# W and R loaded with two tokens of one batch per partition, and the order of the work written anew

## The chip, the cores and the metric

The kernel runs on one core of one Trainium2 chip. A core has five engines that each work through their own list of instructions: TensorE (PE; its weight loads are shown as PEld), VectorE (DVE), ScalarE (ACT), GpSimd (POOL) and SyncE (SP), which here only starts transfers. The metric is the device time of one execution in microseconds (us).

## The reference

The reference is a linear-attention recurrence with a decaying state, followed by a two-layer network with a squared ReLU. For each of 4 batches and 8 heads, with 768 tokens of 40 channels:

```python
for t in range(S):
    y[:, :, t] = np.einsum('bhd,bhde->bhe', rt, state)
    Sa = np.einsum('bhde,bhe->bhd', state, at)
    state_decay = state * wt[:, :, None, :] - np.einsum('bhd,bhe->bhde', Sa, bt)
    state = state_decay + np.einsum('bhd,bhe->bhde', vt, kt)
# x: y with the 8 heads side by side, 3072 tokens x 320
h = x @ w_in                  # 320 x 2048
r = np.maximum(h, 0.0)
out = (r * r) @ w_out         # 2048 x 320
```

Inputs and output are float32.

## The kernel before

The 768 tokens are cut into 6 chunks of 128. A *batch* in the kernel's sense, `m` from 0 to 23, is one chunk of one of the four input batches, with all 8 heads; `m` and `m + 1` with `m` even make a *pair*. A *step* `st` from 0 to 47 is half a batch (4 heads). Inside a chunk the recurrence is solved with matrix products.

**Preparation of a batch** (`add_prep`, L315 to L526). Six loads (W, K, B, A, V, R), from batch 4 on one DMA for a pair (`two`, L296): token t lies on partition t, and each descriptor brings the 40 floats (160 bytes) of one token and head. For batches 0 to 3, R comes in another layout (`rows`, L301), so its transposed copy is read with strides when it is moved out of PSUM (`e_r`, L516). Then:

- `ln` (ACT, L321) takes the logarithm of W into a tile of its own, `hi` scales it by 512 into another, and `lo` takes the float32 minus its upper 16 bits. `cs` (PE, `sums` at L331) forms the sums of the logarithms over the tokens up to each token: two products with a 128 x 128 triangle, one with the upper halves and one with `lo`. `GI` and `GA` (ACT, L356) are the exponentials of minus and plus that sum.
- `E` is `GA` one token earlier. Up to batch 5 (`THREE = 6`) it comes from a second pair of products (`ce`) and an exponential; after that two DMAs shift `GA` by one partition.
- `GL` is the last row of `GA` turned into a column. Up to batch 5 (`GLD = 6`) four one-column products (`gl`, L374) put it into the bank of the sums, and DVE multiplies it out; after that a transposing DMA per pair does it (`gD`, L384), and POOL or DVE multiplies.
- `kb` and `aa` scale K, B and A; `cast` brings V and R to bfloat16; PE turns A, V and R (`tA`, `tV`, `tR`; from batch 8 on K and B are turned by DMA), and ACT or DVE moves each turned block out of PSUM (`AT`, `VT`, `RT`).

**A step** (`add_step`, L539): `ca` (64-row products, L563), masking by DVE (`CN`, L571, twice), `P`, `corr1`, `corr2` with small moves between them (`Mc`, `c1`, `Sn`), `tb`, `ex` (64-row products, L641), masking by DVE (`EVX`, L646, twice), `y` and `Xn`; `us` and `UZ` carry the state to the next chunk.

**The network** (`add_ff`, L800), per batch for the first four and per pair after that: `tx` turns the result, `hr` (64-row, L841) and `hp` (L854) multiply by `w_in`, `hs` applies the ReLU, `Gt` the square, `op` (L888) multiplies by `w_out`, `osb` moves the output, `st` stores it.

**The order.** Nothing is scheduled at run time. The kernel lists its operations, and four tables at the end fix the rest: `ORDER` (L960 on) is the order in which all operations are issued, and so each engine's list; `WAYS` says which of its possible engines an operation uses; `BANKS` gives the PSUM banks; `IDLE` (L1028) names operations of PE ahead of which products without use are put (L1060), in places where PE would otherwise stand idle. Each engine works strictly in order. Ahead of the listed work stand a few clearings of buffers on DVE and POOL (L160 to L209); the other clearings (`blank`, L182) are operations in the list.

## Time and profile before

| what | value |
|---|---|
| median of three runs | 258.16 us (256.76, 258.16, 258.46) |
| time of the profiled execution | 256.97 us |
| its span, first to last instruction | 255.4 us |
| busy PE / DVE / ACT / POOL | 242.0 / 230.4 / 215.6 / 172.0 us |
| granted TensorE clock | 1.000 |
| DMA packets; of these under 512 bytes | 172256; 165047 |

Busy times count an instruction from its start to its modelled end, so neighbours on a pipelined engine overlap: PE's 242.0 us are not 242.0 us of full use. A row of the timeline gives the start, the length from the first start to the last end, the engine and line, the tiles and the count; a row of the groups ends with the busy time, the mean length in nanoseconds and the idle time ahead of the group with what ended it. Starts can be compared directly, and the distance from one start to the next is what an instruction costs its engine when it is never kept waiting.

### The profile page before, as it was taken

How to read it: one execution, taken by the hardware profiler on the slowest of the kernel's cores; microseconds unless marked ns; L12 is line 12 of the kernel's file. 1: busy time of each engine (PE TensorE's matmuls, PEld its weight loads, DVE VectorE, ACT ScalarE, POOL GpSimd, SP SyncE). 2: the span in 40 equal slices, each digit the busy share in tenths (PEclk: the TensorE clock that was granted, in tenths of full speed). 3: DMA queues.
4: the chain of work that ended last, by engine and by line, in shares of the span. 5: the costliest groups of instructions: out<-in, count | busy, mean ns of one | idle time of the engine just before them, and what ended most of it. 6: DMA issues, size and time to landing. Idle time of an engine off the chain costs nothing.

```text
span 255.4 us, 9993 instructions
## 1 busy us (share of the span) xinstructions
PE 242.0 (95%) x3948; PEld 193.1 (76%) x3948; DVE 230.4 (90%) x556; ACT 215.6 (84%) x589; POOL 172.0 (67%) x259
## 2 busy tenths in 40 slices
PE   7978889999999999999999999999999999999993
PEld 7656667787787687887788777877788787878772
DVE  6799999998799999999999999999998898999482
ACT  3669978898698898899999999998999798877660
POOL 4366784886696969875568979995748694716340
PEclk9999999999999999999999999999999999999999
DMA  6999999999599979889988899988898989300111
GB/s 111 189 176 149 174 217 177 147 153 215 101 150 192 168 134 181 173 153 165 200 159 165 160 190 173 167 176 156 154 168 123 214 188 152 70 30 5 68 35 68
DMA packets 172256, 37.95 MB, mean 149 GB/s; under 512 B 165047, under 2 KB 170679, under 8 KB 172206
## 3 DMA queue, kind: packets, MB, share of 16 engines
q1 hardware_dynamic: 169646, 34.66, 76.5%
q0 software_dynamic: 2560, 2.62, 6.2%
q8 instruction: 31, 0.51, 0.9%
q14 instruction: 19, 0.16, 0.2%
HBM read 28.84 MB, written 3.93 MB: 128 GB/s over the span
## 4 chain that ended last, share of the span: by engine, by line
PE 51%; ACT 2%; DVE 2%; DMA 2%; issue 1%; POOL 0%; SPq 0%; POOLq 0%; DVEq 0%
PE bank L888 16%; PE bank L854 10%; PE bank L417 4%; PE bank L641 3%; PE bank L841 3%; PE bank L563 3%; PE bank L595 2%; PE bank L661 2%; DMA NA<-in_a_dram 2%; PE bank L333 1%; PE bank L669 1%; PE bank L623 1%; PE bank L816 1%; PE bank L586 1%; PE bank L628 1%
## 5 line engine op out<-in xcount | busy, mean ns | idle before, releaser
L646 DVE TENSOR_TENSOR EVX<-bank,MEX 128x512 bf16<-128x512 f32 x96 | 62.4, 683 | 1.6 <-PE bank L641 1.1
L571 DVE TENSOR_TENSOR CN<-bank,MCN 128x512 bf16<-128x512 f32 x96 | 61.3, 682 | 1.9 <-PE bank L563 1.0
L888 PE MATMUL bank<-WOUT,Gt 128*128 128x320 bf16 x384 | 59.4, 300 | 0.4 <-DMA WOUT<-in_moe_w_out_dram 0.4
L872 POOL TENSOR_TENSOR Gt<-hs 128x512 bf16<-128x512 bf16 x43 | 45.2, 1055 | 19.2 <-ACT hs L861 14.0
L854 PE MATMUL bank<-XT,WIN 128*128 128x256 bf16 (+1 forms) x448 | 54.5, 258 | 0.0
L861 ACT ACTIVATE hs<-bank 128x512 bf16<-128x512 f32 x77 | 45.5, 601 | 6.0 <-issue 2.5
L888 PEld LDWEIGHTS <-Gt 128*128 128x128 bf16 x384 | 35.4, 97 | 13.3 <-issue 0.8
L854 PEld LDWEIGHTS <-WIN 128*128 128x128 bf16 x448 | 34.8, 97 | 7.1 <-issue 3.6
L612 ACT ACTIVATE junk<-CN 128x512 bf16<-128x512 bf16 x48 | 30.6, 638 | 0.2
L341 POOL TENSOR_TENSOR lo<-hi 128x320 f16<-128x320 f32 x21 | 15.1, 720 | 15.0 <-ACT hi L237 8.5
L401 POOL TENSOR_TENSOR KB<-NB,GI 128x320 bf16<-128x320 f32 (+1 forms) x22 | 18.7, 854 | 8.3 <-ACT GI L357 6.8
L870 ACT ACTIVATE Gt<-hs 128x512 bf16<-128x512 bf16 x37 | 23.1, 636 | 1.4 <-DVE hs L863 1.4
L595 PEld LDWEIGHTS <-CN 128*128 128x128 bf16 x384 | 18.5, 96 | 5.3 <-issue 2.6
L401 POOL TENSOR_TENSOR KB<-NK,GI 128x320 bf16<-128x320 f32 x21 | 18.6, 888 | 5.5 <-ACT GI L357 5.5
L407 POOL TENSOR_TENSOR AA<-NA,E 128x320 bf16<-128x320 f32 x19 | 15.3, 809 | 10.1 <-DMA NA<-in_a_dram 7.5
L563 PE MATMUL bank<-AT,KBT 64*128 64x128 bf16 x384 | 18.0, 218 | 2.2 <-ACT KBT L237 0.7
L841 PE MATMUL bank<-XT,WIN 64*128 64x256 bf16 (+1 forms) x224 | 18.5, 256 | 0.0
L661 PE MATMUL bank<-KB,EVX 128*128 128x40 bf16 x384 | 17.2, 180 | 0.0
L563 PEld LDWEIGHTS <-KBT 64*128 64x128 bf16 x384 | 12.2, 94 | 6.6 <-issue 2.8
L750 POOL TENSOR_TENSOR x<-Mc,c 128x640 bf16<-128x640 bf16 x10 | 14.0, 1398 | 3.9 <-PE bank L641 3.8
L237 ACT ACTIVATE SNall<-bank 128x160 bf16<-128x160 f32 x38 | 11.4, 307 | 6.0 <-PE bank L595 4.5
L681 DVE TENSOR_TENSOR Xn<-bank,E 128x160 bf16<-128x160 f32 x48 | 14.7, 316 | 1.8 <-PE bank L669 0.7
(134 smaller groups left out, 652.6 us busy)
## 6 DMA issues: line engine op xcount, KB each, us to landing
out_dram<-osb SPq DMA_DIRECT2D x24, 160.0 KB, 2.4
NW<-in_w_dram SPq DMA_DIRECT2D x10, 320.0 KB, 4.5
NK<-in_k_dram SPq DMA_DIRECT2D x10, 320.0 KB, 5.5
NB<-in_b_dram SPq DMA_DIRECT2D x10, 320.0 KB, 5.1
NA<-in_a_dram SPq DMA_DIRECT2D x10, 320.0 KB, 5.2
NV<-in_v_dram SPq DMA_DIRECT2D x10, 320.0 KB, 5.3
NR<-in_r_dram SPq DMA_DIRECT2D x10, 320.0 KB, 4.9
E<-GA SPq DMA_DIRECT2D x9, 224.0 KB, 4.6
```

The source lines that it names most:

```text
L401: engine(eng).tensor_tensor(out=o.KB.tile[:, u, h, 0:D], in0=o.nat[key].tile[:, m % 2, h], op=ALU.mult, in1=o.GI.tile[:, h])
L563: nc.tensor.matmul(out=quads(ca[s])[:, i, u, :], lhsT=o.KBT.tile[half(s), u, j0 + i, :], rhs=o.AT.tile[half(s), j0 + i, :], start=(i == 0 ...
L571: nc.vector.tensor_tensor(out=t_[:, :, s], in0=quads(ca[s]), in1=MCN[:], op=ALU.mult)
L595: nc.tensor.matmul(out=P[:, 2 * i + s], lhsT=CN[:, i, s, 1, :], rhs=X[:, 2 * i + s], start=False, stop=last, skip_group_check=True)
L612: nc.scalar.activation(out=t_, in_=CN_.tile[:, :, :, 1, :], func=ACTF.Square, accum_out=ACC[:, AN + st:AN + st + 1])
L646: nc.vector.tensor_tensor(out=sb(EV_, [128, 2, 2, 2, L], BF16)[:, :, s], in0=quads(ex[s]), op=ALU.mult, in1=MEX[:].rearrange("p (i u) x -> ...
L841: nc.tensor.matmul(out=hv(w_)[:, u], lhsT=WIN[2][half(w_), j * 128:(j + 1) * 128], rhs=XT()[half(w_), 2, 0:nb, :], start=(u == 0), stop=False,
L854: nc.tensor.matmul(out=hv(w_)[:, u], lhsT=WIN[g][:, (j0 + u) * 128:(j0 + u + 1) * 128], rhs=XT()[:, g, 0:nb, :], start=False, stop=(g == 1 ...
L861: nc.scalar.activation(out=t_, in_=hpb.tile[:], func=ACTF.Relu)
L870: nc.scalar.activation(out=t_, in_=x_, func=ACTF.Square)
L872: engine(eng).tensor_tensor(out=t_, in0=x_, in1=x_, op=ALU.mult)
L888: nc.tensor.matmul(out=opb.tile[:, 0:DM], lhsT=Gtb[h].tile[:, j, b_, :], rhs=WOUT[:, j, :], start=(j == 0), stop=(j == NJ - 1))
```

## The change

From batch 4 on (`TWOS = 4`), the fifth batch onward:

- **Layout of W and R.** `twos` replaces `two` for these two inputs. Partition `64 z + i` holds tokens `2i` and `2i + 1` of batch `z` of the pair. A descriptor brings 320 bytes in place of 160, and each pair's load is two DMAs of 64 partitions in place of one of 128.
- **Logarithms per pair.** `ln`, `hi` and `lo` are one instruction each for the pair (640 elements per partition in place of two times 320). The logarithm and its scaling are written into W's own tile; the rings `lnW` and `hi` are gone, and W's ring has three tiles in place of two.
- **Sums by 64-row products.** `cs` is one operation per pair: eight 64-row products of 320 columns in place of four of 128 rows. The triangles are the new constants `UP`, one for even and one for odd tokens, in both number types.
- **R** is cast once per pair, turned by eight products into one bank that the pair shares, and moved out in a strided read that interleaves even and odd tokens again.

Beside that:

- `GL` comes from the one-column products in all 24 batches; the transposing DMA (`gD`) is gone.
- `E` is shifted by DMA from batch 4 on in place of batch 6 (`THREE = 4`).
- Clearings may go to POOL, and those of `UZ` touch only the padding.
- `BY_DMA` gains ranges that start at 24, past the last batch: no transpose moves to DMA.
- `ORDER`, `WAYS`, `BANKS` and `IDLE` are new. Read out, they give this:

| operation | engines before | engines after |
|---|---|---|
| `VT` | ACT 12, DVE 13 | ACT 18, DVE 7 |
| `Mc` | ACT 32, DVE 16 | ACT 39, DVE 9 |
| `hs` | ACT 77, DVE 19 | ACT 80, DVE 16 |
| `XT` | ACT 12, DVE 12 | ACT 8, DVE 16 |
| `GL` | DVE 10, POOL 14 | DVE 24 |
| `Gt` | ACT 37, DVE 16, POOL 43 | ACT 39, DVE 17, POOL 40 |
| `hi` | ACT 14, DVE 10 | ACT 7, DVE 7 (of 14) |
| `lo` | DVE 3, POOL 21 | DVE 2, POOL 12 (of 14) |
| cast of R | ACT 11, DVE 4, POOL 9 | ACT 3, DVE 1, POOL 10 (of 14) |
| `x1` and `Cc` | DVE 5, POOL 19 | POOL 24 |
| `RT` | ACT 21, DVE 3 | ACT 21, DVE 3 |
| clearings in the list | DVE 14, POOL 7 | DVE 8, POOL 15 |

PE's list goes over from 128-row products to 64-row products 87 times before and 76 times after (64-row products are `ca`, `ex`, `hr`, the turning of R in batches 0 to 3, and, after, `cs` of the pairs), and comes back as often. The products without use ahead of PE's operations are 84 before and 104 after; 47 of the 104 stand ahead of `tA` of batch 4 and 8 ahead of `ca` of step 8. Batch 0's W is the first load after the change and the second before; W's logarithm and sums of batch 0 stand ahead of those of batch 1 after the change and behind them before. At its start DVE's list has, ahead of the first `hi`, two clearings of `KB` after the change, and six clearings before (two `KB`, one each of `V`, `UZ`, `R` and `GA`).

```diff
-    RING = {"N": 3, "NW": 2, "lnW": 2, "GI": 2, "KB": 5, "GA": 2, "E": 3, "AA": 2, "V": 5, "R": 3, "SN": 8,
-            "EVX": 3, "RT": 4, "VT": 4, "KBT": 3, "AT": 3, "GL": 4, "GD": 2, "CN": 3, "c1": 2, "x1": 2,
+    RING = {"N": 3, "NW": 3, "GI": 2, "KB": 5, "GA": 2, "E": 3, "AA": 2, "V": 5, "R": 2, "SN": 8,
+            "EVX": 3, "RT": 4, "VT": 4, "KBT": 3, "AT": 3, "GL": 4, "CN": 3, "c1": 2, "x1": 2,
             "Mc": 2, "Cc": 2, "TB": 9, "UZ": 2, "us": 2, "Xn": 3, "XT": 3, "hs": 3, "Gt": 2, "osb": 3,
-            "hi": 2, "lo": 2}
+            "lo": 2}
     NBANK = 8
-    SPLIT, THREE, ROWS, GLD, PAIR = 1, 6, 4, 6, 4
+    SPLIT, THREE, ROWS, PAIR, TWOS = 1, 4, 4, 4, 4
...
+    UP = {(x, i): gl.tile([128, 128], BF16 if i == 0 else FP16, name=f"UP{x}{i}") for x in range(2) for i in range(2)}
...
-    def blank(ring, i):
+    def blank(ring, i, eng="DVE"):
+        fill = nc.gpsimd if eng == "POOL" else nc.vector
+        if ring == "UP":
+            for x in range(2):
+                for b_ in range(2):
+                    nc.gpsimd.affine_select(
+                        out=UP[x, i][64 * b_:64 * b_ + 64], in_=ones_b[64 * b_:64 * b_ + 64], pattern=[[1, 128]],
+                        compare_op=ALU.is_ge, fill=0.0, base=-x, channel_multiplier=-2,
+                    )
+            return
...
+        if ring == "UZ":
+            t_ = t_[:].rearrange("p i (s d) -> p i s d", s=2)
+        fill.memset(t_[..., D:64], 0.0)
...
+            op(("blank", ring, i), "DVE", rank, 0.01 + 0.00104 * n, 0.03 + 0.00104 * n, [], [],
+               lambda eng, ring=ring, i=i: blank(ring, i, eng),
+               alts=[("POOL", 0.04 + 0.00075 * n, 0.1 + 0.0007 * n)])
...
-    BY_DMA = {"KB": range(8, NBC), "V": (), "A": ()}
+    BY_DMA = {"KB": range(8, NBC), "V": range(24, NBC), "A": range(24, NBC), "X": range(24, NBC)}
...
+        o.lo, o.R, o.b4 = ((bt[m - 1].lo, bt[m - 1].R, bt[m - 1].b4) if m >= TWOS and m % 2
+                           else (buf("lo"), buf("R"), buf("bank", "prep")))
+        o.csb = buf("bank", "prep")
...
+        def twos():
+            for z in range(2):
+                nc.sync.dma_start(
+                    out=tile_()[half(z)].rearrange("p b h e -> p (b h e)").rearrange("p (h x) -> p h x", x=2 * D),
+                    in_=nat_srcs[key][bb + z, :, c * L:(c + 1) * L, :].rearrange("h (i s) e -> i h (s e)", s=2))
...
-           two if m >= PAIR else rows if key == "R" and m < ROWS else go)
+           twos if m >= TWOS and key in "WR" else pair if m >= PAIR else rows if key == "R" else go)
...
         def ln():
-            t_ = sb(o.lnW, [128, NHH * D], FP32)
-            nc.scalar.activation(out=t_[:], in_=o.nat["W"].tile[:, m % 2].rearrange("p h e -> p (h e)"),
-                                 func=ACTF.Ln)
-        op(("ln", m), "ACT", s0 - 3.2, *act(320), [("L", m, "W")], [o.nat["W"], o.lnW], ln)
-        csb = buf("bank", "prep")
-
-        def upper(t_):
-            return t_[:].bitcast(BF16).rearrange("p (x y) -> p x y", y=2)[:, :, 1]
+            nc.scalar.activation(out=logs(), in_=logs(), func=ACTF.Ln)
...
+        def sums2():
+            for i, rhs in enumerate((upper(), o.lo.tile[:])):
+                rows_ = rhs.rearrange("p (h s e) -> p s h e", s=2, e=D)
+                for x in range(2):
+                    for z, b_ in enumerate((bt[m - 1].csb, csb)):
+                        nc.tensor.matmul(out=heads(b_.tile[:, 0:NHH * D]), lhsT=UP[x, i][half(z), :],
+                                         rhs=rows_[half(z), x], start=(i == 0 and x == 0),
+                                         stop=(i == 1 and x == 1))
...
+        if twin and m % 2 == 0:
+            for x in ("ln", "hi", "lo", "cs"):
+                alias[x, m] = x, m + 1
+        else:
+            op(("ln", m), "ACT", s0 - 3.2, *act(320 * wide_), [("L", m, "W")], [o.nat["W"]], ln)
+            op(("hi", m), "ACT", s0 - 3.15, *act(320 * wide_), [("ln", m)], [o.nat["W"]], hi,
+               alts=[("DVE", 0.25 * wide_, 0.32 * wide_)])
+            op(("lo", m), "POOL", s0 - 3.0, 0.663 * wide_, 0.72 * wide_, [("hi", m)], [o.nat["W"], o.lo], lo,
+               alts=[("DVE", 0.4 * wide_, 0.48 * wide_)])
...
+        if not twin:
+            op(("cs", m), "PE", s0 - 2.9, *pe(0.27), [("lo", m)], [o.nat["W"], o.lo, csb], lambda: sums("I", csb), "F")
+        elif m % 2:
+            op(("cs", m), "PE", s0 - 2.9, *pe(0.56), [("lo", m), *(("blank", "UP", i) for i in range(2))],
+               [o.nat["W"], o.lo, bt[m - 1].csb, csb], sums2, "R")
...
-        def gl_row():
-            nc.sync.dma_start_transpose(out=sb(o.GD, [128, 2 * PB, 32], BF16)[:],
-                                        in_=o.GA.tile[96:128].rearrange("p b h e -> p (b h e)"))
-        if m < GLD:
-            op(("gl", m), "PE", s0 - 0.5, *pe(0.102), [("GA", m), ("GI", m)], [o.GA, csb], gl_mm, "F")
-            op(("GL", m), "DVE", s0 - 0.3, 0.075, 0.16, [("gl", m)] + cleared("HM", 0), [csb, o.GL],
-               lambda: gl_ev("DVE", csb.tile[:, 320:320 + PB]))
-        else:
-            if m % 2:
-                op(("gD", m), "SP", s0 - 2.0, 0.6, 0.6, [("GA", m - 1), ("GA", m)], [o.GA, o.GD], gl_row)
-                ops["gD", m].dma = "h", 0.4
-                alias["gD", m - 1] = "gD", m
-            op(("GL", m), "POOL", s0 - 0.3, 0.1, 0.16, [("gD", m)] + cleared("HM", 0), [o.GD, o.GL],
-               lambda eng: gl_ev(eng, o.GD.tile[:, PB * (m % 2):PB * (m % 2) + PB, 31]), alts=[("DVE", 0.075, 0.16)])
+                in0=csb.tile[:, 320:320 + PB].rearrange("p (j u) -> p j u", u=1).to_broadcast([128, PB, 2]))
+        op(("gl", m), "PE", s0 - 0.5, *pe(0.102), [("GA", m), ("GI", m)], [o.GA, csb], gl_mm, "F")
+        op(("GL", m), "DVE", s0 - 0.3, 0.075, 0.16, [("gl", m)] + cleared("HM", 0), [csb, o.GL], gl_ev)
...
+        def cast_r(eng):
+            if twin:
+                copy(eng, out=o.R.tile[..., 0:D],
+                     in_=o.nat["R"].tile[:].rearrange("p b h e -> p (b h) e").rearrange("p (h s) e -> p s h e", s=2))
...
+            if twin:
+                turn(bank(b4), [flat(o.R.tile[:, x, 2 * j:2 * j + 2, :]) for x in range(2) for j in range(PB)])
                 return
...
+            if twin:
+                copy(eng, out=t_.rearrange("p j (i s) -> p j i s", s=2),
+                     in_=bank(b4)[:, 0:2 * PB * L].rearrange("p (s j b i) -> p b j i s", s=2, j=PB, b=2)[:, m % 2])
...
+        elif m % 2:
+            op(("tR", m), "PE", s0 - 0.6, *pe(0.444), [("cast", m, "R", 0)], [o.R, b4, bt[m - 1].RT, o.RT], t_r, "F")
...
-    IDLE = ((135, 29, 7), (42, 8, 1), (44, 23, 2), (90, 10, 0), (329, 6, 0), (929, 8, 5),)
+    IDLE = ((34, 19, 7), (44, 13, 1), (62, 5, 4), (176, 4, 6), (183, 8, 3), (406, 47, 0), (413, 8, 5),)
```

258 lines of the change are left out of this document (134 added, 124 removed).

## The prediction

> **What bounds the kernel now.** I read the page first, then the busy times by stage, then PE's timeline row by row.
>
> ```profile
> span 255.4 us, 9993 instructions
> PE 242.0 (95%) x3948; PEld 193.1 (76%) x3948; DVE 230.4 (90%) x556; ACT 215.6 (84%) x589; POOL 172.0 (67%) x259
> ```
> ```profile
> 8.00:16.00 8.00, 6.86 (x111) 4.97 (x106) 6.48 (x15) 6.54 (x23) 4.93 (x14) 1.00 0.99 176
> 16.00:32.00 16.00, 13.23 (x271) 10.18 (x270) 15.06 (x41) 13.82 (x43) 9.76 (x16) 1.00 1.00 167
> 32.00:64.00 32.00, 29.36 (x566) 24.04 (x565) 29.96 (x72) 27.95 (x73) 22.92 (x30) 1.00 1.11 182
> ...
> 128.00:160.00 32.00, 31.95 (x521) 25.55 (x518) 30.44 (x77) 30.90 (x91) 26.07 (x39) 1.00 0.90 171
> ```
>
> The second fence gives, per stage, its length, then the busy time of PE, PEld, DVE, ACT and POOL, the clock, the DMA share and GB/s. PE is full in the middle, but DVE (95% of 128 to 160) and ACT (97%) are nearly so. Busy PE is not PE at its peak, so I went to its starts.
>
> ```profile
> 131.32 0.30 PE L333 MATMUL bank<-lo,UTI 128*128 128x320 f16 x1
> 131.46 0.60 PE L854 MATMUL bank<-XT,WIN 128*128 128x256 bf16 x4
> 131.99 0.29 PE L641 MATMUL bank<-RT,VT 64*128 64x128 bf16 x4
> ...
> 132.22 0.39 PE L563 MATMUL bank<-AT,KBT 64*128 64x128 bf16 x8
> 132.45 0.43 PE L841 MATMUL bank<-XT,WIN 64*128 64x256 bf16 x4
> 132.81 0.61 PE L854 MATMUL bank<-XT,WIN 128*128 128x256 bf16 x4
> 133.26 1.25 PE L888 MATMUL bank<-WOUT,Gt 128*128 128x320 bf16 x8
> 134.34 0.60 PE L854 MATMUL bank<-XT,WIN 128*128 128x256 bf16 x4
> 134.87 0.39 PE L841 MATMUL bank<-XT,WIN 64*128 64x256 bf16 x4
> 135.10 0.39 PE L563 MATMUL bank<-AT,KBT 64*128 64x128 bf16 x8
> ```
>
> These rows follow each other without a pause: a product of 320 columns costs 0.14 us (131.32 to 131.46), four of 256 columns 0.45 (132.81 to 133.26), eight 64-row products of 128 columns 0.23 (132.22 to 132.45), and four 64-row products of 256 columns 0.23 (134.87 to 135.10). Where the kind changes there is a step. Four 256-column products take 0.53 when 64-row ones follow (131.46 to 131.99 and 134.34 to 134.87): 0.08 more than 0.45. Four 64-row products take 0.36 when 128-row ones follow (132.45 to 132.81): 0.13 more than 0.23. I take 0.1 us a change.
>
> ```profile
> 1.36 2.96 PE L174 MATMUL bank<-ones_b 128*128 128x128 bf16 x26 [1.36 <-DVE ones_b L160]
> ...
> 248.00 3.43 PE L888 MATMUL bank<-WOUT,Gt 128*128 128x320 bf16 x24
> ```
>
> With such spacings for every form I went through PE's 992 timeline rows, of which these are the first and the last. PE works 207.7 us (the last row's 3.4 included), pays 17.4 for 174 changes of kind, and stands 25.0 in real gaps: 12.3 before 40 us, 6.0 from 40 to 96, 6.7 after that. With 1.4 ahead of its first product, 4.0 behind its last and 1.6 outside the span, that makes the profiled execution's 256.97 to within 0.2. So from 40 us on PE's own list nearly sets the time, and only the start has much to give. The median of the runs is 1.2 above the profiled execution; I add that at the end.
>
> **PE's list, part by part.** *Sums:* four products of 0.14 a pair are 0.56; eight 64-row ones, if two run side by side as in L563 (eight of 128 columns in 0.23; at 0.14 for 320 columns, one after the other would need 8 x 0.056 = 0.45), are 8 x 0.14 / 2 = 0.56. Nothing changes. *E by shift:* two batches less of `ce`, 4 x 0.14 = 0.56 saved.
>
> ```profile
> 14.72 0.34 PE L376 MATMUL bank<-IDb,GA 128*128 128x1 bf16 x8
> ```
> ```profile
> L376 PE MATMUL bank<-IDb,GA 128*128 128x1 bf16 x24 | 1.3, 165 | 0.0
> ```
>
> *GL by products:* 18 batches more, 72 products. Eight span 0.34 with a tail of 0.165, so 0.025 each; 1.3 / 24 = 0.054 is the upper end. That is 1.8 to 3.9; I take 1.8, since they stand in a full list. *Changes of kind:* 87 runs of 64-row products become 76, although ten operations join the kind; 22 changes x 0.1 = 2.2 saved. The turning of R (eight products a pair) costs the same. Sum on PE: -0.56 + 1.8 - 2.2 = **-1.0**; by the upper price of GL, +1.1. [...] If each change cost the whole tail of a product, 165 ns by the row of L376, 22 changes would give 3.6 and the sum would be -2.4; the two measured steps, 0.08 and 0.13, lie below that tail, so I stay at 0.1.
>
> **The start.**
>
> ```profile
> 3.67 0.59 SPq L292 DMA_DIRECT2D NA<-in_a_dram  x1
> ...
> 4.03 0.47 ACT L323 ACTIVATE lnW<-NW 128x320 f32<-128x320 f32 x1 [1.71 <-DMA NW<-in_w_dram]
> ...
> 4.10 0.43 DVE L190 MEMSET KB<- 128x192 uint32 x2
> ...
> 4.79 0.91 DVE L198 MEMSET UZ<- 128x1024 uint32 x1 [0.16 <-issue]
> ...
> 5.94 0.26 DVE L242 TENSOR_SCALAR hi<-lnW 128x320 f32<-128x320 f32 x1
> ...
> 8.62 0.30 PE L333 MATMUL bank<-lo,UTI 128*128 128x320 f16 x1
> ...
> 9.25 0.56 DVE L407 TENSOR_TENSOR AA<-NA,E 128x160 bf16<-128x160 f32 x2 [1.32 <-ACT E L352]
> ...
> 12.51 0.40 PE L563 MATMUL bank<-AT,KBT 64*128 64x128 bf16 x8
> ```
>
> The first logarithm is ready at 4.50, but `hi` waits until 5.94 behind clearings on DVE, and batch 0's sums end with the product at 8.62, since batch 1 goes first. With two clearings of KB ahead (to 4.53), and batch 0 first, `hi` starts near 4.55, `lo` ends near 5.2, and the sums end some 3.3 us earlier. What is late next is the data: A is issued at 3.67, in both orders among the first six loads, and lands about 4 us later (3.4 by the 160 KB row below, and the queue is fuller here), so `aa` gains about 1.2 (9.25 to 8.0) and the first `ca` (12.51) 1 to 3. Not all of that stays: from 8 to 32 us the DMA share is 0.99 and 1.00 and DVE is 94% busy (15.06 of 16), and the loads of batches 0 to 3 are unchanged in size. There is also a new wait. `tA` of batch 4 now needs the pair's sums, both `GA` and the shift:
>
> ```profile
> E<-GA SPq DMA_DIRECT2D x9, 224.0 KB, 4.6
> ```
>
> 4.6 us to landing, where `E` came straight from a product before. Behind this wait PE's whole list stands; the 47 + 8 products without use put there (0.056 each by the same reckoning) stand for 3.1 us of idle time. On SP the shift waits for both `GA`, with the load of W for batches 6 and 7 queued behind it; on PE the useful work left behind `tA` of batch 4 differs by only 0.4 us between the two orders. Between 0 and -3 for the first and 0 to +3 for the second, net I take **-1.5** for the first 40 us: the old start has 12.3 us of gaps, and three of them are named.
>
> **Relief behind the start.**
>
> ```profile
> L240 DVE COPY VT<-bank 128x512 bf16<-128x512 bf16 x12 | 5.0, 416 | 0.1
> ...
> L240 DVE CAST Mc<-bank 128x160 bf16<-128x160 f32 x16 | 5.0, 318 | 1.0 <-PE bank L586 0.9
> ...
> L863 DVE TENSOR_SCALAR hs<-bank 128x512 bf16<-128x512 f32 x19 | 12.8, 684 | 2.8 <-ACT junk L765 2.4 <-PE bank L854 0.2
> ...
> L381 DVE TENSOR_TENSOR GL<-bank,HM 128x8 f32<-128x8 f32 x6 | 0.9, 156 | 0.0
> ```
> ```profile
> L237 ACT ACTIVATE RT<-bank x21: 586/597/654, 8.3 to 231.8; 128x512 bf16<-128x512 bf16 x21
> L240 DVE COPY RT<-bank x3: 415/420/685, 43.5 to 223.6; 128x512 bf16<-128x512 bf16 x3
> ```
>
> DVE loses six `VT` (-2.5), seven `Mc` (-2.2), three `hs` (-2.1) and two whole clearings of UZ (-1.8 by the 0.91 above), and gains 14 `GL` (+2.2). `RT` is the strided read: the slowest of the three on DVE, 0.685, is batch 3 in the old strided layout, the other two 0.415 and 0.420 are not; so +0.27 for each of the three, one of which was strided already: +0.5. On ACT the longest of 21 is 0.654 against 0.597, so 0 to +0.06 each. The other moves of the table go both ways, none with more than four instructions, and none longer than `hs`; I take them at 0, +-2. DVE: -6 of 230.
>
> ```profile
> L323 ACT ACTIVATE lnW<-NW 128x320 f32<-128x320 f32 x24 | 11.3, 478 | 1.9 <-DMA NW<-in_w_dram 1.9
> ...
> L765 ACT ACTIVATE junk<-Mc 128x640 bf16<-128x640 bf16 x12 | 8.9, 738 | 0.0
> ```
>
> On ACT a logarithm of 640 elements should take about 0.74 (the other 640-element row), against 2 x 0.478: ten pairs save 2.2, `VT` adds 6 x 0.6 = 3.6 (its block has the shape of `RT`, 0.597), seven `Mc` more and eight casts of R fewer roughly cancel. ACT stays where it was, and it was as full as DVE. So a lighter DVE can only take away part of the 12.7 us of gaps after 40 us: 0 to -4, I take **-1.0**. The saved transfers buy nothing by themselves: the row of L323 shows 1.9 us of waiting for W in the whole span, all of it at the start (1.71 of it is in the row at 4.03).
>
> Sum: -1.0 - 1.5 - 1.0 = -3.5, so 253.5 for an execution like the profiled one, and **254.6** against the median of 258.16 (-1.4%).
>
> **The rivals.** *The gains at the start are given back at batch 4* (the shift): the new wait of 3.1 takes the place of the gaps removed, and ACT holds the middle. Then only PE's -1.0 and a little remain: -1, 257.2. For it: the planted products, and a DMA share of 1.11 from 32 to 64 in which the shift must land. Against it: this wait lies where the old list had gaps too.
>
> *The chain of the logarithms, now per pair, is longer than its lead* (slower). `ln` 0.26 and `hi` 0.26 longer than for one batch, the sums 0.28, and `lo` on POOL:
>
> ```profile
> L341 POOL TENSOR_TENSOR lo<-hi 128x320 f16<-128x320 f32 x21 | 15.1, 720 | 15.0 <-ACT hi L237 8.5 <-DVE hi L242 6.4
> ```
>
> 0.72 longer if twice as long. That is 1.5 us per pair before the first batch of the pair can go on. It is hidden as long as preparation runs ahead of its step by more than that; it decides from about four uncovered pairs (4 x 1.5 - 3.5 = +2.5). With five: +4, 262.2. For it: ACT and POOL are the engines that `lo` waits for. Against it: no PE wait in the old trace is on `lo` beyond a few tenths.
>
> ```profile
> NW<-in_w_dram SPq DMA_DIRECT2D x4, 160.0 KB, 3.4
> NR<-in_r_dram SPq DMA_DIRECT2D x8, 80.0 KB, 3.3
> ```
>
> The loads in halves belong to the same rival: a half-height load of 80 KB lands in 3.3 us, hardly faster than one of 160 KB (3.4), so if the two halves came one after the other, W would be 2 us later still. [...]
>
> *The 64-row sums do not run side by side*: ten times 8 x 0.14 - 0.56 = 0.56, +5.6 on PE's list; 253.5 + 5.6 + 1.2 = 260.3.
>
> *Everything falls into place*: the start keeps 3 and the later gaps lose 4: 250.2.
>
> **How the numbers follow.** Forecast 0.50, gains given back 0.25, long chain 0.11, serial sums 0.05, everything 0.09. Faster by over 1% is below 255.6, slower above 260.7; a smaller change can't be told from none here. The forecast's own range, 252.5 to 257, lies four fifths in faster: 0.40, with 0.09 from the last case and 0.01 from the second: 0.50. Within 1%: 0.10 + 0.23 + 0.03 = 0.36. Slower: 0.11 from the chain, 0.02 from the serial sums and 0.01 from the second case, 0.14. Range 251.0 to 260.0: it leaves out about half of the last case, nearly all of the long chain and part of the serial sums.
>
> **What would show it.** Right: the first `ca` before 11.5 us; PE with 152 changes of kind; the eight sums in about 0.6; DVE's busy sum near 224; a PE gap near 40 us of at most 3. Wrong: PE idle on `GA`, `KBT` or `AT` again and again in the middle, or a later start of the first `ca`.

## The result, and the profile after

The changed kernel is slower: 264.63 us median of four runs (263.02 to 265.16) against 257.46 (256.60 to 258.46), ratio 1.0271 [1.0234, 1.0308]. The profiled execution took 264.69 us. Ratios, here and below, leave out executions that lie far above a kernel's fastest, so the medians, which count all, stand beside them. Forecast were 254.6, and 251.0 to 260.0 as the range: wrong in size and in sign.

From the page of the kernel after, the span, the busy times and the granted clock in 40 slices (before, the clock was 9 in every slice):

```profile
span 263.1 us, 10268 instructions
...
PE 243.6 (93%) x4076; PEld 198.1 (75%) x4076; DVE 221.9 (84%) x544; ACT 218.1 (83%) x575; POOL 181.4 (69%) x251
...
PEclk9997997999999999999799999999999999999999
```

The stages that the prediction showed, in the same columns, from the kernel after:

```profile
8.00:16.00 8.00, 7.21 (x126) 5.31 (x126) 6.59 (x19) 6.17 (x21) 4.36 (x9) 1.00 0.89 164
16.00:32.00 16.00, 13.32 (x253) 10.40 (x254) 13.67 (x33) 13.67 (x40) 12.78 (x25) 0.89 0.97 173
32.00:64.00 32.00, 26.85 (x547) 23.61 (x545) 24.80 (x60) 22.64 (x62) 20.33 (x23) 0.95 1.02 172
128.00:160.00 32.00, 31.97 (x537) 25.81 (x535) 29.50 (x74) 29.85 (x79) 24.62 (x32) 0.98 1.13 167
```

From 32 to 64 us PE lost 2.5 us (26.85 for 29.36), DVE 5.2 and ACT 5.3: all three stand idle more than before, so none of them is the bound there. The transfers go at nearly the pace they had (172 GB/s, 182 before). What all wait for stands in PE's timeline, kernel after; the brackets give the idle time and what ended it:

```profile
19.23 0.40 PE L455 MATMUL bank<-IDb,V 128*128 128x128 bf16 x4 [1.67 <-POOL V L253]
...
36.53 0.38 PE L455 MATMUL bank<-IDb,KB 128*128 128x128 bf16 x4
39.65 0.40 PE L455 MATMUL bank<-IDb,KB 128*128 128x128 bf16 x4 [2.74 <-POOL KB L431]
...
46.02 2.79 PE L1115 MATMUL bank<-ones_b 128*128 128x128 bf16 x47
48.64 0.39 PE L455 MATMUL bank<-IDb,AA 128*128 128x128 bf16 x4
...
104.42 0.40 PE L611 MATMUL bank<-AT,KBT 64*128 64x128 bf16 x8 [1.13 <-DMA KBT<-KB]
...
124.62 0.25 PE L643 MATMUL bank<-c,CN 128*128 128x40 bf16 x4 [1.86 <-DVE c L656]
...
256.01 3.43 PE L945 MATMUL bank<-WOUT,Gt 128*128 128x320 bf16 x24
```

Before, no wait of PE behind its start reached 1 us; here are three of 1.7 to 2.9 us (counted from the end of the work ahead; the bracket counts a little less). The second is the largest: K of batch 4 is there and turned at 36.53, and B, scaled on POOL, comes 3 us later. POOL's timeline and the chain of waits of the kernel after say why:

```profile
38.73 0.86 POOL L431 TENSOR_TENSOR KB<-NB,GI 128x320 bf16<-128x320 f32 x1 [2.99 <-DMA NB<-in_b_dram]
```
```profile
28.62 10.04 DMA NB<-in_b_dram
...
46.18 2.62 PE bank L1115 x47
...
120.64 3.12 DMA E<-GA
```

POOL waits for the load of B for batches 4 and 5, which was 10 us under way. Now the list of transfers on SP: first the kernel before, with the row of POOL that takes B up there without waiting and PE's turning of K and B of batch 4, then the kernel after (`NB` of 320 KB at L297 and L313 is B of batches 4 and 5, `NV` the V of the same two):

```profile
25.94 1.17 SPq L297 DMA_DIRECT2D NB<-in_b_dram  x1
...
37.20 3.51 SPq L297 DMA_DIRECT2D NV<-in_v_dram  x1
```
```profile
35.48 1.68 POOL L401 TENSOR_TENSOR KB<-NB,GI 128x320 bf16<-128x320 f32 x2
```
```profile
37.94 0.61 PE L417 MATMUL bank<-IDb,KB 128*128 128x128 bf16 x8
```
```profile
24.28 1.22 SPq L313 DMA_DIRECT2D NV<-in_v_dram  x1
25.54 2.41 SPq L326 DMA_DIRECT2D NR<-in_r_dram  x2
28.00 0.58 SPq L313 DMA_DIRECT2D NK<-in_k_dram  x1
28.62 2.02 SPq L313 DMA_DIRECT2D NB<-in_b_dram  x1
```

In the new order V of batches 4 and 5 is asked for 12.9 us sooner, ahead of B, and B is asked for 2.7 us later. PE's turning of V of batch 4 comes only 2.8 us sooner (44.81 for 47.60), and it comes to the turning of K and B 1.4 us sooner (36.53 for 37.94). The old B was 9.1 us under way and was taken up 9.5 us after its issue, so it was hardly faster than the new one (10.0); it had been asked for in time.

**A second loss follows each long wait.** The windows of one microsecond of the kernel after (columns as above; the last three are the clock, the DMA share and GB/s):

```profile
20.00:21.00 1.00, 1.00 (x17) 0.82 (x12) 0.75 (x3) 1.00 (x4) 1.00 (x3) 0.50 0.61 139
...
41.00:42.00 1.00, 1.00 (x14) 1.00 (x13) 1.00 (x4) 1.00 (x3) 1.00 (x2) 0.50 0.75 96
42.00:43.00 1.00, 1.00 (x22) 1.00 (x19) 0.02 (x1) 0.85 (x2) 1.00 (x2) 0.50 0.95 187
...
126.00:127.00 1.00, 1.00 (x10) 0.87 (x9) 1.00 (x3) 0.35 (x1) 1.00 (x2) 0.50 0.98 169
```

Behind the waits of 1.7, 2.9 and 2.0 us the granted clock is 0.50 for some 3.4 us each (from 19.7, 40.2 and 125.6), worth up to 1.7 us apiece. Behind those of 1.3 us (44.75, 104.42) it stays at 1.00.

**Where the time went**, by PE's starts. My count of the old list had a slip: it took 64-row products of 256 columns for 128 columns, which put 4.5 us of work down as gaps. Mended, with the same prices for both kernels, up to the start of the last row of the network:

| us of PE | before | after |
|---|---|---|
| work (of it products without use) | 208.8 (6.3) | 209.8 (7.2) |
| changes of kind x 0.1 | 174: 17.4 | 152: 15.2 |
| gaps, 0 to 48 | 12.9 | 18.3 |
| gaps, 48 to 96 | 4.9 | 1.4 |
| gaps, 96 to 128 | 0.9 | 6.1 |
| gaps, after 128 | 1.7 | 3.8 |
| ahead of the first product | 1.4 | 1.4 |
| last row starts | 248.0 | 256.0 |

Half clock shows as gaps in this count. The gaps grow by 9.2 us and PE's list shrinks by 1.2; that makes the loss of 8.0 us.

### The profile page after: what moved, and what is told of

The parts are those of the page before. It is cut to its first block, busy times and chain, and to the rows that moved or that the text cites. A ratio compares the mean times of both kernels' runs of the same rounds, so it can differ in the third digit from the quotient of the medians.

```text
span 263.1 us, 10268 instructions
## 1 busy us (share of the span) xinstructions
PE 243.6 (93%) x4076; PEld 198.1 (75%) x4076; DVE 221.9 (84%) x544; ACT 218.1 (83%) x575; POOL 181.4 (69%) x251
## 4 chain that ended last, share of the span: by engine, by line
PE 64%; SPq 12%; DMA 9%; DVE 5%; ACT 4%; issue 2%; POOL 1%; DVEq 0%; ACTq 0%
PE bank L945 17%; PE bank L911 14%; SPq L308 6%; PE bank L455 5%; DMA NB<-in_b_dram 4%; PE bank L611 4%; PE bank L898 4%; PE bank L689 3%; PE bank L709 3%; SPq L326 3%; PE bank L643 3%; DMA E<-GA 3%; PE bank L717 2%; SPq L319 2%; DMA NW<-in_w_dram 1%
## 5 line engine op out<-in xcount | busy, mean ns | idle before, releaser
L619 DVE TENSOR_TENSOR CN<-bank,MCN 128x512 bf16<-128x512 f32 x96 | 62.1, 681 | 4.6 <-PE bank L611 3.7
L929 POOL TENSOR_TENSOR Gt<-hs 128x512 bf16<-128x512 bf16 x40 | 41.8, 1049 | 24.2 <-ACT hs L918 19.4
L911 PE MATMUL bank<-XT,WIN 128*128 128x256 bf16 (+1 forms) x448 | 55.3, 260 | 0.0
L431 POOL TENSOR_TENSOR KB<-NB,GI 128x320 bf16<-128x320 f32 (+1 forms) x23 | 19.8, 863 | 10.0 <-ACT GI L399 5.3
L927 ACT ACTIVATE Gt<-hs 128x512 bf16<-128x512 bf16 x39 | 24.3, 632 | 1.0 <-DVE hs L920 0.8
L643 PEld LDWEIGHTS <-CN 128*128 128x128 bf16 x384 | 19.4, 97 | 5.9 <-issue 3.6
L798 POOL TENSOR_TENSOR x<-Mc,c 128x640 bf16<-128x640 bf16 x12 | 17.0, 1414 | 7.7 <-ACT Gt L927 6.1
L374 POOL TENSOR_TENSOR lo<-NW 128x640 f16<-128x640 f32 (+1 forms) x12 | 14.0, 1166 | 6.3 <-PE bank L911 3.0
L656 DVE TENSOR_TENSOR c<-bank,Mc 128x160 bf16<-128x160 f32 x48 | 14.6, 316 | 3.5 <-PE bank L643 3.1
L709 PE MATMUL bank<-KB,EVX 128*128 128x40 bf16 x384 | 17.4, 181 | 0.0
L802 POOL TENSOR_TENSOR Cc<-x,SNall 128x640 bf16<-128x640 bf16 x12 | 17.0, 1415 | 0.0
```

Of the source, the lines that this page charges most:

```text
L431: engine(eng).tensor_tensor(out=o.KB.tile[:, u, h, 0:D], in0=o.nat[key].tile[:, m % 2, h], op=ALU.mult, in1=o.GI.tile[:, h])
L619: nc.vector.tensor_tensor(out=t_[:, :, s], in0=quads(ca[s]), in1=MCN[:], op=ALU.mult)
L643: nc.tensor.matmul(out=P[:, 2 * i + s], lhsT=CN[:, i, s, 1, :], rhs=X[:, 2 * i + s], start=False, stop=last, skip_group_check=True)
L709: nc.tensor.matmul(out=Y[:, 2 * i + s], lhsT=EV_.tile[:, i, s, u, :], rhs=o.KB.tile[:, u, head(i, s), 0:D], start=first, stop=(u == 1 and ...
L911: nc.tensor.matmul(out=hv(w_)[:, u], lhsT=WIN[g][:, (j0 + u) * 128:(j0 + u + 1) * 128], rhs=XT()[:, g, 0:nb, :], start=False, stop=(g == 1 ...
L929: engine(eng).tensor_tensor(out=t_, in0=x_, in1=x_, op=ALU.mult)
```

## The experiments

All ran against the kernel before, whose median was 257.37 to 257.69. Theory A puts the loss on the loads in halves; theory D says that the early part is paced by the transfers and the new order asks for data out of step with that. The executions of the kernel before lie 2.5 to 4.2 us apart in a comparison; those of the kernel after lay 2.1 us apart, but with some of its loads moved they lie up to 9.3 us apart. SP's and other lists in the diffs are read out of `ORDER`.

**Are the half-height loads at fault?** One run takes them out of the kernel after, one puts them into the kernel before; both mix up the tokens of W and R.

```diff
-           twos if m >= TWOS and key in "WR" else pair if m >= PAIR else rows if key == "R" else go)
+           pair if m >= PAIR else rows if key == "R" else go)
```

> The changed kernel with W and R loaded as before the change: one DMA of 128 partitions with 160-byte pieces, one token of both batches to a partition. The rest, order and arithmetic, is the changed kernel's, so the sums and the reads of R take their tokens in the wrong order: what is left out is the right pairing of the tokens, no work. Theory A (the loads in halves hold up the SP queue and the transfers behind them): the time falls most of the way, to 257 to 260. Theory B (the loss is made by the order: three places where PE waits over 1.5 us, each followed by about 3 us at half clock): the waits stay, 263 to 267.

Measured: 264.71, 1.0261 [1.0194, 1.0328]. The wait at batch 4 stays, from PE's timeline of this run:

```profile
39.48 0.61 PE L455 MATMUL bank<-IDb,KB 128*128 128x128 bf16 x4 [2.75 <-POOL KB L431]
```

```diff
...
-           two if m >= PAIR else rows if key == "R" and m < ROWS else go)
+           twos if m >= PAIR and key in "WR" else two if m >= PAIR else rows if key == "R" and m < ROWS else go)
```

> The kernel before with W and R of batches 4 to 23 loaded as after the change (two DMAs of 64 partitions, 320-byte pieces), nothing else changed: tokens come out in the wrong order, no work is left out. Theory A: the halves hold up the queue, 260 to 264. Theory B: within 1 us of the kernel before.

Measured: 257.35, 0.9981 [0.9946, 1.0016]. The halves cost nothing and bring nothing, in either order. Theory A falls.

**Are the fillers or the clock at fault?**

```diff
-    IDLE = ((34, 19, 7), (44, 13, 1), (62, 5, 4), (176, 4, 6), (183, 8, 3), (406, 47, 0), (413, 8, 5),)
+    IDLE = ((34, 19, 7), (44, 13, 1), (62, 5, 4), (176, 4, 6), (183, 8, 3),)
```

> The changed kernel without the 47 and 8 products without use ahead of the turning of A of batch 4 and of step 8. In the profile AA of batch 4 was ready at 45.9 when they started at 46.0. Theory B1 (PE comes there late, so they are paid in full): 55 x 0.056 = 3.1 less, 261 to 262.5. Rival (PE would wait there anyway, and without them its clock falls): no change, or up to 2 us more.

Measured: 263.83, 1.0242 [1.0155, 1.0328]. Step 8's `ca` came 3 us sooner in the profiled execution (46.66 for 49.61), and under 1 us of that is left in the median. Two more runs put fillers ahead of the waits instead, to keep the clock up:

```diff
-    IDLE = ((34, 19, 7), (44, 13, 1), (62, 5, 4), (176, 4, 6), (183, 8, 3), (406, 47, 0), (413, 8, 5),)
+    IDLE = ((34, 19, 7), (44, 13, 1), (62, 5, 4), (176, 4, 6), (183, 8, 3), (151, 30, 4), (408, 45, 3), (927, 22, 4), (975, 33, 5),)
```
```diff
-    IDLE = ((34, 19, 7), (44, 13, 1), (62, 5, 4), (176, 4, 6), (183, 8, 3), (406, 47, 0), (413, 8, 5),)
+    IDLE = ((34, 19, 7), (44, 13, 1), (62, 5, 4), (176, 4, 6), (183, 8, 3), (151, 36, 4), (408, 75, 3), (975, 36, 5),)
```

151 is the turning of V of batch 1, 408 that of K and B of batch 4, 975 `corr2` of step 22 (the three long waits), 927 `ca` of step 21.

> The changed kernel with those 55 products taken away and others put where PE really stood: 30 ahead of the turning of V of batch 1, 45 ahead of the turning of K and B of batch 4, 22 ahead of ca of step 21, 33 ahead of corr2 of step 22. Clock theory (a wait over about 1.7 us is followed by some 3 us at half clock, 1.5 us lost each): granted clock 1.00, and three times 1.5 less on top of the 3.1 at batch 4: 256 to 259. Rival (the low clock costs nothing, since PE waits for others anyway): 261 to 263, as without the products at batch 4, or more where the new ones come in the way.

> As e4_fill_moved, with more products without use where PE stood: 36 ahead of the turning of V of batch 1, 75 ahead of the turning of K and B of batch 4, 36 ahead of corr2 of step 22, none at the turning of A of batch 4 and at ca of steps 8 and 21. Clock theory: if they last as long as the waits, the clock stays at 1.00 and the three stretches at half clock go, 1.5 us each: 259 to 261. Rival (PE is short of data anyway, so a slow PE loses nothing): 263 to 264, as e3_no_fill, with the clock at 1.00 all the same.

Measured: 263.9, 1.0202 [1.0129, 1.0274], and 263.48, 1.0249 [1.0184, 1.0313]. In the second the mean clock was 0.993 (0.979 in the kernel after) and no slice after 40 us fell below 9; the time hardly moved. It is no clean price of the half clock, though. The 75 products ahead of K and B met half clock themselves, from 35.9 to 39.3:

```profile
36.38 5.73 PE L1115 MATMUL bank<-ones_b 128*128 128x128 bf16 x75
```

They kept PE until 41.95; in the kernel after, B was ready at 39.59 (38.73 and 0.86 on POOL). Clearer is a run further down (the network's weights late): its profiled execution has a single stretch of half clock, behind the first wait, and a mean clock of 0.992, and still took 261.76. So the half clock is not the main loss.

**Does one late load make that loss?** The kernel before, with only the load of B for 4 and 5 moved:

```diff
-SP: B 4/5, A 4/5, R 3, W 6/7, V 4/5
+SP: A 4/5, R 3, W 6/7, B 4/5, V 4/5
```

> The kernel before with only B of batches 4 and 5 moved back on SP, behind R of batch 3 and W of batches 6 and 7: issued near 37 us in place of 26. Clock theory: PE waits 3 to 5 us ahead of the turning of K and B of batch 4, then runs at half clock for about 3 us, and the granted clock of the run falls to 0.98 or 0.99; the time rises by the wait and about 1.5, to 261 to 264. Rival (a single late load is taken up by the slack behind it): under 1 us.

Measured: 263.24, 1.0235 [1.0220, 1.0250]. PE's timeline of this run:

```profile
37.94 0.38 PE L417 MATMUL bank<-IDb,KB 128*128 128x128 bf16 x4
43.39 0.61 PE L417 MATMUL bank<-IDb,KB 128*128 128x128 bf16 x4 [5.06 <-POOL KB L401]
```

One load 8.2 us later (issued 34.13 for 25.94) makes a wait of 5.2 us and costs 5.9. Behind the wait PE works until 48.6 at half clock, worth up to 2.6 us more. So the wait, or most of it, reaches the end, for there is little slack in PE's list behind 40 us.

**Then put the load earlier.** In the kernel after, B is put ahead of V; then the same with three loads of the middle moved as well (B 10/11 and W 12/13 sooner, W 18/19 behind the shift of `E` for 12/13); then all of these and two at the start (V 1 ahead of R 1, W 3 behind both). The diff is of the first:

```diff
-SP: V 4/5, R 3, K 4/5, B 4/5, A 4/5
+SP: B 4/5, V 4/5, R 3, K 4/5, A 4/5
```

> The changed kernel with one load moved on SP: B of batches 4 and 5 goes two places ahead of its V instead of behind K, so it is issued about 4 us earlier, ahead of the weights of the network. Theory B (waits for single late transfers, each with its stretch of half clock, make the loss): the wait of 2.9 us ahead of the second half of the turning of K and B of batch 4 goes, and the half clock behind it: 2.9 + 1.5 less, 259 to 261, if nothing else is late there by then. Rival C (batch 4 is late on several inputs at once, the shift of E and A as well): the wait moves behind the planted products, under 1.5 us gained, 263 to 264.5.

> As e5_b4_early, and three more moves on SP in the middle: B of batches 10 and 11 ahead of the turning of batch 9, W of batches 12 and 13 ahead of A of batches 10 and 11, and W of batches 18 and 19 behind the shift of batch 13. Theory B: the waits at 104 us (1.4) and 124 us (2.0, with its half clock) go too: 4 to 5 less than e5_b4_early, 255 to 257. Rival C (the preparation as a whole is too late, and each wait taken away shows the next): 1 to 2 less than e5_b4_early.

> As e6_sp_four, and at the start V of batch 1 ahead of its R, and W of batch 3 behind both, so that V is issued 2.5 us earlier. Theory B: the wait of 1.7 us ahead of the turning of V of batch 1 goes, and the half clock from 20 to 23 us: 2 to 3 less than e6_sp_four. Rival C: the first 40 us are limited by all loads together, 0 to 1 less.

Measured: medians 265.44 (261.30 to 265.55), 266.74 with ratio 1.0369 [1.0335, 1.0403], and 266.44 (260.42 to 269.04); the first and the third without an interval. From the waits of PE in the first (28 to 50 us; columns: total, times, longest):

```profile
PE bank L556 <- ACT R L250: 3.7, 1, 3.7
PE bank L455 <- POOL KB L431: 0.8, 1, 0.8
```

The wait has moved from B to a load that B overtook, R of batch 3. The load pulled up pushed another behind its time, and PE waits 3.7 us for that one. The loads of W in the middle, by themselves:

```diff
-SP: W 12/13 and W 14/15 in their places, W 18/19 ahead of W 16/17
+SP: W 12/13 and W 14/15 exchanged with the loads of R of the same batches, W 18/19 behind W 16/17
```

> The changed kernel with the loads of W of batches 12 to 15 moved forward on SP to where those of R stood, R moved back in turn, and W of batches 18 and 19 moved back behind W of 16 and 17. Theory F (in the middle the transfers that start a pair's chain stand behind loads that are not yet needed): the waits at 104 and 124 us (1.4 and 2.0) and the half clock behind the second go, 260 to 262. Rival C: they move elsewhere, 263 to 265.

Measured: 263.25, 1.0229 [1.0161, 1.0297], 1.4 less in the median; the wait at batch 4 was 4.4 us in its profiled execution.

**Is it the transfers' pace?** Both kernels without the loads of V and R for batches 1 and 3 (they use those of 0 and 2). No work of the other engines is left out, but SP has six transfers fewer to start.

```diff
...
-           twos if m >= TWOS and key in "WR" else pair if m >= PAIR else rows if key == "R" else go)
+           (lambda: None) if key in "VR" and m in (1, 3) else twos if m >= TWOS and key in "WR" else pair if m >= PAIR else rows if key == "R" else go)
...
```

> The changed kernel without four of the first loads: V and R of batches 1 and 3 are left out, those of batches 0 and 2 are used in their place. Theory D (up to 45 us the DMA engines set the pace, and the new order asks for the data of batches 1 to 4 earlier than it can come): 640 KB less are 3.9 us at the 165 GB/s of that stage; the wait at batch 4 and its half clock go, 257 to 260. Rival E (the loss is made in the order behind that, by late preparation in the middle): 263 to 265.

> The kernel before without the same four loads. Theory D: it has no long wait there, so it gains less than the changed kernel, 1 to 3: 254.5 to 256.5. Rival E: the two kernels gain alike.

Measured: the kernel after 256.37, 0.9955 [0.9901, 1.0008]; the kernel before 257.53, 1.0000 [0.9956, 1.0044]. The same bytes (four loads of 160 KB, 3.8 us at 172 GB/s) are worth 8.3 us to the new order, a little more than theory D asked, and nothing to the old, where it asked for 1 to 3. The windows of the kernel after without these loads:

```profile
0.00:48.00 48.00, 41.84 (x732) 34.54 (x733) 39.52 (x104) 35.35 (x102) 34.20 (x71) 0.96 0.99 171
...
96.00:128.00 32.00, 30.98 (x536) 24.91 (x534) 29.86 (x78) 29.89 (x79) 26.06 (x32) 1.00 1.05 182
```

and of the full one:

```profile
0.00:48.00 48.00, 37.13 (x628) 30.39 (x629) 36.00 (x95) 33.28 (x95) 33.26 (x69) 0.93 0.93 169
...
96.00:128.00 32.00, 28.63 (x456) 22.36 (x453) 26.57 (x66) 26.97 (x72) 24.14 (x28) 0.96 1.10 177
```

The pace is equal (171 and 169 GB/s). With less to bring, B of batches 4 and 5 is asked for at 24.38 and lands 5.4 us later, PE is busy 4.7 us more in the first 48 us, and the waits of the middle are gone as well (but for the one that ended at 8.28, none of PE behind its start is over 0.9 us). So the loss goes back to the first loads, which come at 164 and 173 GB/s (8 to 16 and 16 to 32 us of the kernel after) in a sequence that is too late for the new order. Three things the run leaves open. It takes away the load that PE waited for at 19.23. It doesn't tell the pace of the DMA engines from the time that SP spends on starting transfers. And whether lateness at the start always makes the waits of the middle isn't shown: in the run with the network's weights late, PE no longer waits for B of batch 4, but the wait near 124 us is still there (2.4 us).

**Is it their sequence alone?** All bytes kept: V of 4 and 5 put where the old order had it, behind B; or two loads of the network's first weights (`WIN`, the expert weights of the expectations) put behind B; or both; or both with the loads of W from the run with W early and without the fillers.

```diff
-SP: V 4/5, R 3, K 4/5, B 4/5, A 4/5, shift of E 4/5
+SP: R 3, K 4/5, B 4/5, A 4/5, V 4/5, shift of E 4/5
```

> The kernel after, with the load of V for batches 4 and 5 (320 KB) put behind the loads of A for 4 and 5 in SP's order, so behind the load of B that TensorE waits for near 37 us, and its two conversions put later on ScalarE. In the kernel before, that V was asked for behind B, at 37.2 us; in the kernel after it is asked for at 24.3 us, ahead of B (28.6 us). Theory D (the early part is paced by the transfers, and the new order asks for V, R and W ahead of what TensorE needs next): 320 KB by 169 GB/s is 1.9 us, so the wait of 2.9 us at the turning of K and B of batch 4 falls to about 1.0, the half clock behind it goes too, and the time is 259.5 to 261.5 us. Rival (what is needed by batch 4 is fixed, so a load moved back only moves the wait to another place, as when B alone was pulled ahead): 263 to 265.5 us.

```diff
-POOL: WIN 2, WIN 1, cast V 3, x1, K 4, K 5, B 4, copy of Xn, WIN 0
+POOL: cast V 3, x1, K 4, K 5, B 4, WIN 2, WIN 1, copy of Xn, WIN 0
```

> The kernel after, with two of the three loads of the first expert weights (384 KB, issued on GpSimd at 29.7 and 30.9 us, right behind B's) put behind the products of B of batch 4 on GpSimd. Theory D: 384 KB by 169 GB/s is 2.3 us less beside B's load, the wait at batch 4 falls from 2.9 to about 1 us, the clock stays up, and the first products of these weights (45.2 us) may wait up to 1 us: 259.5 to 262 us. Rival (the wait only moves): 263 to 265.5 us.

> Both moves of the two runs ahead together. Theory D: 4.2 us of transfers are out of the way of B's load, no wait over 1 us at batch 4, clock at full rate until 100 us, time 256.5 to 260 us. Rival: 262.5 to 265 us, with a wait of 2 us or more at another load ahead of 60 us.

> Both moves, the loads of W for batches 12 to 18 in the earlier places of the run with W early, and the 55 filling products behind batch 4 left out. Theory D: as with both moves, less what the 55 fillers cost (about 1 to 3 us) and the waits between 96 and 128 us (up to 3 us): 253.5 to 257.5 us. Rival: 261.5 to 264 us.

Measured, in this order: 263.1 (257.71 to 266.61), 1.0189 [1.0099, 1.0279]; 262.16, 1.0143 [1.0062, 1.0223]; 262.02, 1.0178 [1.0100, 1.0257]; 263.93, 1.0214 [1.0133, 1.0296]. Against 264.63 the first three gain 1.5 to 2.6 us in the median, less than theory D asked: the first falls into its rival's range, the second just outside the range of theory D, the third 2.0 us above it. The fourth gains 0.7 and falls into its rival's range too, with new waits of 1.9 us for V of batch 1 and 2.1 us at 43 us in its profiled execution (by the brackets). What theory D says of batch 4 holds: the profiled execution with V late took 257.71, and its timelines of SP and PE show no wait for B, since all eight products of K and B run as one group:

```profile
26.33 1.32 SPq L313 DMA_DIRECT2D NB<-in_b_dram  x1
```
```profile
36.93 1.01 PE L455 MATMUL bank<-IDb,KB 128*128 128x128 bf16 x8
```

But its other three executions took 262 to 267. Two more runs asked why: V late with V of batch 1 ahead of R of batch 1 and W of 3 later, then that without the 55 fillers.

> The kernel with V of batches 4 and 5 late, and also the two moves at the start that the run with six moves had (the load of V of batch 1 ahead of R of batch 1, and W of batch 3 behind the loads of batch 2), which are there to take away the wait for V of batch 1 near 17 us (1.7 us, with half clock behind it). Theory D with the clock: without that wait the clock stays full to 40 us (about 1.6 us saved) and the wait at batch 4 stays away: median 259 to 261.5 us, and a spread between runs no wider than 5 us. Rival (the first loads have no order that serves all; the wait goes to R of batch 1 or to batch 2): 262 to 264.5 us.

> The same with the 55 filling products behind batch 4 left out, since their wait is gone with V late. Theory D: 1 to 3 us off the run with the fillers, 257 to 260 us. Rival: within 1 us of the run with the fillers, because what ends the wait there is not TensorE's own work but the chain over VectorE and GpSimd.

Measured: 263.37 (257.54 to 266.88), 1.0063 [1.0024, 1.0101], and 265.6 (259.73 to 266.93), without an interval: both far from what theory D asked. The wait near 17 us was down to 0.3 and 0.6 us, the spread was not. The profiled execution of the first took 266.88, and its timelines of SP, ACT and PE show where it waited:

```profile
31.28 6.39 SPq L313 DMA_DIRECT2D NV<-in_v_dram  x1
```
```profile
43.62 0.47 ACT L250 ACTIVATE V<-NV 128x320 bf16<-128x320 f32 x1 [3.55 <-DMA NV<-in_v_dram]
```
```profile
44.14 0.60 PE L455 MATMUL bank<-IDb,V 128*128 128x128 bf16 x4 [2.75 <-ACT V L250]
```

Now V is the late one: 12.3 us from issue to use, where the profiled execution with V late alone had it by 40.3 (issued at 30.5). The profiled execution without the fillers (266.93) waits 3.8 us at the same place. So of three profiled executions, the one in which batch 4's data came in time took 257.71, and the two in which V came too late took 266.9. That the other executions spread for the same reason is likely and not shown, since they left no trace; nor is the share of the clock, which was 0.50 for 6.8 and 10.2 us around these two waits. What makes a given transfer 2 us quicker in one execution than in the next was not found, and no order tried beats the median of the kernel before. No run puts the logarithms and sums per pair into the old order, so what they would bring by themselves stays open.

## Why the prediction was wrong

**The start (-1.5) is the step that failed most.** Between the forecast sum of -3.5 and the +8.0 of the table lie 11.5 us: 6.9 of them are here (+5.4 for -1.5) and 4.8 in the relief (+3.8 for -1.0); PE's list gave 0.2 more than forecast. The first half of the step held in the profiled execution: the first `ca` starts 1.5 us sooner, forecast 1 to 3. From the kernel after:

```profile
10.98 0.40 PE L611 MATMUL bank<-AT,KBT 64*128 64x128 bf16 x8
```

Even this gain isn't sure: in five of the sixteen profiled executions of the new order, all five with loads moved or left out (in one of them only behind 80 us), that `ca` starts at 12.3 to 12.6, no sooner than before (12.51), with half clock from about 9 to 13 us.

The second half of the step asked for the new wait in the wrong place. I put 0 to +3 us on the shift of `E` ahead of `tA` of batch 4. That wait is not what PE met: it met B of batch 4, 3 us, some nine microseconds sooner. I had both halves of the argument in hand (DMA share 0.99 and 1.00 from 8 to 32 us, and the new `ORDER`). I used the first only to discount the gain, and did not use the second: the loads of batches 0 to 3 keep their size, I wrote, but I did not read in which sequence SP asks for those of 4 and 5, nor set that against PE's new list. The gaps to 48 us came out at +5.4, where -1.5 were forecast for the first 40. That the late load makes such a loss, the run with B late in the kernel before shows (5.9 us).

**"The saved transfers buy nothing by themselves" fell short.** It was true of W, the one input I looked at, and of the halves (both runs). But the row of L323 cannot speak for an order that asks for other data sooner. The four loads left out bought 8.3 us.

**Relief behind the start (-1.0).** DVE fell by 8.5 us (230.4 to 221.9; forecast about 224), and from 48 to 96 us the gaps fell by 3.5, near the far end of "0 to -4". Then the middle gave back 5.2 from 96 to 128 and 2.1 after that, on waits for transfers again: a DMA transpose of `KBT` at 104.42, and `E` of batch 12, whose shift stood on SP behind two loads (the second `GA` of the pair was done at 117.1, the shift began at 119.26). From SP's and DVE's timelines, kernel after:

```profile
114.24 2.46 SPq L313 DMA_DIRECT2D NB<-in_b_dram  x1
116.81 2.36 SPq L319 DMA_DIRECT2D NW<-in_w_dram  x2
119.26 1.96 SPq L409 DMA_DIRECT2D E<-GA  x2
```
```profile
123.84 0.49 DVE L437 TENSOR_TENSOR AA<-NA,E 128x320 bf16<-128x320 f32 x1 [2.22 <-DMA E<-GA]
124.25 0.32 DVE L656 TENSOR_TENSOR c<-bank,Mc 128x160 bf16<-128x160 f32 x1
```

DVE stood in order at `AA` for a batch to come, with `c` of the running step behind it, and PE behind `c` for 2.0 us. With the mended count the gaps after 40 us had been smaller than the 12.7 I offered as the reserve, too: about 2.6 and not 6.7 after 96.

**PE's list (-1.0) held.** There are 152 changes of kind for 174, -2.2 by my price. The eight sums and the change behind them take 0.72 from the first to the next operation of another kind, so about 0.6, as forecast:

```profile
30.07 0.51 PE L366 MATMUL bank<-NW,UP 64*128 64x320 bf16 x4
30.36 0.50 PE L366 MATMUL bank<-lo,UP 64*128 64x320 f16 x4
30.79 0.28 PE L671 MATMUL bank<-IDb,SNall 128*128 128x128 bf16 x2
```

I left out that 20 more products without use cost 0.9; with these the list is -1.2 by the table (work +1.0, changes -2.2).

**The rivals.** "Given back at batch 4" had the right place, the wrong transfer, and too low a price: it let the wait replace gaps and end at 257.2, while a late load ran through to the end (5.2 us of wait, 5.9 of time, with B late in the kernel before). "The chain of logarithms" is not seen: no long wait of PE is on `lo` behind its start. "Serial sums" is refuted by the rows above. Of the signs for wrong, idle PE on `KBT` in the middle did show. All five signs for right came out too (10.98 us, 152 changes, 0.6, 221.9, and a gap near 40 us of 2.9), which says that they were badly chosen: none of them was on a load, I had no price for the clock, and a gap of 3 us that is new is not one of the old gaps.

**The clock.** Ahead of PE's last products the stretches at a granted clock of 0.50 lasted 3.4 us or near a multiple of that: 3.4 us three times in the kernel after (from 19.7, 40.2 and 125.6), 6.8 and 10.2 us around the waits for V in the last two runs, and some 17 us, to about 50, in the first run with B early (mean clock 0.959). What sets these lengths is not shown. Nor does the length of a wait alone decide whether one follows. An idle gap of 1.7 us was followed by one at 19.23. In the run without the four loads, 1.4 us (ended 8.28) were followed by half clock from 9.3 to 12.8. In the run with the network's weights late, the same wait as at 124.62 was longer (2.19 for 1.86 by the brackets), and the clock stayed at 1.00, as PE's timeline and the windows of that run show.

```profile
123.83 0.25 PE L643 MATMUL bank<-c,CN 128*128 128x40 bf16 x4 [2.19 <-DVE c L656]
```
```profile
125.00:126.00 1.00, 1.00 (x18) 0.97 (x16) 1.00 (x4) 0.57 (x2) 1.00 (x2) 1.00 0.91 147
126.00:127.00 1.00, 1.00 (x27) 0.90 (x26) 0.85 (x3) 1.00 (x4) 0.96 (x1) 1.00 1.30 295
```

## What to carry to other kernels

Where the DMA share is near 1.0 (from 16 to 32 us 1.00 in the kernel before and 0.97 in the one after), an order of work is also an order of bytes: list the loads as the queue issues them, with the time each takes to land under load, beside the starts of their first users, for the order before and the order after. A new wait of PE in a full list cost its whole length here (5.2 us of wait, 5.9 of time, with B late in the kernel before), and 3.4 us at a clock of 0.50 behind it are worth up to 1.7 us more; in the kernel after, the work saved elsewhere did not hide it. An order whose data come just in time must be judged by several executions: the best of eleven here was 257.54 and their median 263.37.

## What was not expected of the hardware

- Three waits of PE of 1.7, 2.9 and 2.0 us were followed by 3.4 us at a clock of 0.50 each (from 19.7, 40.2 and 125.6 us in the kernel after), but the length of one wait does not decide it: two of 1.3 us in the same run and one of 2.4 us in another were not followed by it, one of 1.4 us in a third was, and in the profiled execution with V late the clock was 0.50 from 35.6 to 39.0 where no wait in the 5 us ahead reached 0.5 us.
- A load of 320 KB took 10 us from issue to landing at a DMA share of 1.03 (`NB`, 28.62 to 38.7), where the median of its group over the whole execution is 5.9.
- Two loads of 64 partitions in pieces of 320 bytes take the place of one load of 128 partitions in pieces of 160 without any clear change in time (0.9981 [0.9946, 1.0016], in the kernel before).
- The strided read on DVE took longer than the plain one of the same size: `RT` 0.686 us for `VT` 0.411 in the kernel after; I had taken this from a single instruction, and it holds for all three (0.674 to 0.692):

```profile
L253 DVE COPY VT<-bank 128x512 bf16<-128x512 bf16 x7 | 2.9, 411 | 0.0
...
L253 DVE COPY RT<-bank 128x512 bf16<-128x512 bf16 x3 | 2.1, 686 | 0.5 <-ACT RT L250 0.4
```
